# A gelu that waits for VectorE moves behind a seed copy, and convolution items are dealt out otherwise

## The chip, the cores and the metric

The kernel runs on one NeuronCore of a Trainium2 chip. The metric is the device time of one execution in microseconds; the median of three runs is given. The engines that matter here are TensorE (PE in the profile, with PEld for its weight loads), ScalarE (ACT), VectorE (DVE) and SyncE (SP), which issues most transfers.

## The reference

A causal convolution along the sequence, seven taps, with one softmax-normalised set of taps for each of eight groups of 24 channels, is followed by a two-layer network with a quick gelu between its layers:

```python
# x: (8, 4096, 192), weight: (8, 7), w_in: (192, 2048), w_out: (2048, 192)
w = softmax(weight, axis=-1)
out[b, s, h, :] = sum_k w[h, k] * x_pad[b, s + k, h, :]   # 6 zero rows ahead
h = out.reshape(32768, 192) @ w_in
g = h * (1.0 / (1.0 + np.exp(-1.702 * h)))
return g @ w_out
```

## The kernel before

The 32768 tokens are worked on in 32 blocks ("big"), each of which serves two steps `s` (64 steps, numbered from 0). Step 0 is written out by itself and also prepares the weights; the loop runs steps 1 to 63. Both matrix products are done blockwise with seven products in place of eight (a scheme of Strassen's kind), so sums and differences of blocks are formed before and after the products. In the loop a step has two units `a` and `b` (halves of the hidden columns). A unit's products p1 to p7 go to PSUM tiles: `x` and `z` are two of three rotating slots, and `sums` is one tile that both units share.

```python
# cut: inside class Unit
def p1(self):    self.pe(self.x, W11, C11, True)
def seed(self):  act.copy(sums, self.x)             # ScalarE: PSUM to PSUM
def p6(self):    self.pe(sums, X2, V2)              # accumulates on the seed
def keep2(self): self.u2 = ...; act.copy(self.u2, sums)
def p5(self):    self.pe(self.z, X1, V1, True)
def p5b(self):   self.pe(self.z, W23, C32)
def p7(self):    self.pe(sums, X3, V3)
def keep3(self): self.u3 = ...; act.copy(self.u3, sums)
def p2(self):    self.pe(self.x, W12, C21); self.pe(self.x, W13, C31)
def h11(self):   self.gelu(B11, self.x)
def p4(self):    self.pe(sums, W22, V4); self.pe(sums, W23, C31)
def h21(self):   self.gelu(B21, sums)               # reads sums: p4 must be done
def add22(self): vec.tensor_add(self.u3, self.u3, self.z)
def h22(self):   self.gelu(B22, self.u3)            # add22 must be done
def p3(self):    self.pe(self.z, X4, C22); self.pe(self.z, X5, C32)
def add12(self): vec.tensor_add(self.u2, self.u2, self.z)
def h12(self):   self.gelu(B12, self.u2)
def sum_g(self, i): ...                             # VectorE: differences of gelus
```

The convolution of a coming block is done on VectorE between the other operations. It is a list of small items, and `work(n)` takes the next n of them from the list (all of them for None):

```python
def prepare(big):
    for c in range(NC):                  # NC = 3
        yield lambda c=c: transpose_x(big, c)
    if big + 1 < N_BIG:
        yield lambda: load_x(big + 1)
    yield lambda: new_f(big)
    for c in range(NC):
        for k in range(K):               # K = 7; k = 0 is the cheaper form
            yield lambda c=c, k=k: conv(big, c, k)
    for i in range(4):
        yield lambda i=i: sums_c(big, i)
    yield lambda: cross(big)             # a transfer between halves of f
```

The loop, cut to the parts that matter (`nxt` is the first unit of the coming step, whose p1 and seed are done ahead from step 2 on):

```python
for s in range(1, N_ST):
    a, b = nxt or Unit(s, 0), Unit(s, 1)
    if nxt is None:                      # steps 1 and 2
        a.p1(); a.seed(); a.p5(); a.p5b(); a.p6(); a.keep2()
        a.p2(); a.h11(); a.p7(); b.p1(); a.keep3()
    else:
        a.p6(); a.keep2(); a.p2(); a.h11(); a.p7(); a.keep3(); a.p5(); a.p5b()
    nxt = ...
    work(4 if s > 1 else 9)
    a.add22(); a.h22(); a.p4(); a.h21()
    if s > 2: b.p1()
    b.seed(); a.p3()
    work(None if s % 2 and s > 1 else 2)
    a.add12(); b.p5(); b.p6(); b.keep2(); a.h12()
    b.p2(); b.p7(); b.keep3(); b.h11()
    if nxt: nxt.p1()
    b.p5b()
    work(1 if s > 1 else 2)
    a.sum_g(0); a.sum_g(1)
    b.add22(); b.p4(); b.h21(); b.h22()
    if nxt: nxt.seed()
    b.p3(); a.sum_g(2); a.sum_g(3); b.add12(); b.h12()
    if s == 1: work(1)
    if s % 2 and (s + 3) // 2 < N_BIG:
        todo += prepare((s + 3) // 2)
    output(s, b, work)
```

`output` does the second multiplication: five products of 32 matmuls and one of eight "quarters", with `work(2)`, `work(2)`, `work(3)` and `work(3)` between its parts. Its last part, with its lines in the profile:

```python
    work(3)
    p7, p4c = product2(ra, 0, (S3, T3), (A22, T4, 1))    # L476
    act.copy(chunk(p4, 1), p4c)                          # L566
    vec.tensor_add(u1, u1, p7)                           # L567
    vec.tensor_add(u2, u2, p7)                           # L568
    out.turn(1, 1, u1)
    vec.tensor_sub(u2, u2, p4)                           # L570
    out.turn(1, 0, u2)
    out.store()
```

In step 2 the PSUM slot `ra` of step 1's output is the `z` that a's p5 writes.

Of the kernel before, what the change touches and what calls it, by code (L numbers as in the profile page):

```python
# [15 lines left out]
def kernel(  # L16
# [45 lines left out]
    N_BIG = (B // 2) * CHUNKS  # L62
# [27 lines left out]
    def load_x(big):  # L90


        p, c = divmod(big, CHUNKS)
        xin = xins[big] = xin_pool.tile([P, 2, NJ, XW], F32, name="xin")
        if c == 0:
            nc.gpsimd.memset(xin[0:R, :, 0, :], 0.0)
        for o in range(2):
            j = 1 if c == 0 and o == 0 else 0
            t = c * TOK + o * T + (j - 1) * Q
            for v in range(2):  # L100
                q0 = o * R + v * Q
                for n in range(2):
                    nc.sync.dma_start(
                        out=xin[q0 : q0 + Q, n, j:NJ, :],
                        in_=x_v[n, p, t : t + (NJ - j) * Q, v * Q : v * Q + XW].rearrange(
                            "(j i) d -> i j d", i=Q
                        ),
                    )
# [213 lines left out]
    def transpose_x(big, c):  # L322
        if big not in xts:
            xts[big] = xt_pool.tile([P, NC, 2, XT], F32, name="xt")
        vec.transpose(
            xts[big][:, c, :, :].rearrange("p n (j t) -> p (n j) t", t=Q),
            xins[big].rearrange("p n j d -> p (n j) d")[:, :, c * R : c * R + Q],
        )
        if c == NC - 1:
            xins.pop(big)  # L330
# [4 lines left out]
    def conv(big, c, k):  # L335
        src = conv_src(big, c, k)
        dst = fs[big][:, 0, 2 * c : 2 * c + 2, :]
        tap = cw[:, c, k : k + 1]
        if k == 0:
            vec.tensor_scalar_mul(dst, src, tap)  # L340
        else:
            vec.scalar_tensor_tensor(  # L342
                out=dst, in0=src, scalar=tap, in1=dst, op0=ALU.mult, op1=ALU.add
            )

    def sums_c(big, i):
        f = [fs[big][:, 0, j, :] for j in range(NB)]
        dst, a, b = [(V1, C12, C11), (V3, C22, C12), (V2, C22, V1), (V4, C21, V2)][i]
        vec.tensor_sub(f[dst], f[a], f[b])

    def cross(big, b0=0, b1=NB, queue=nc.sync):

        f = fs[big]
        for o in range(2):
            queue.dma_start(out=f[halves[1 - o], 1, b0:b1, :], in_=f[halves[o], 0, b0:b1, :])

    def new_f(big):
        fs[big] = f_pool.tile([P, 2, NB, T], F32, name="f")
# [9 lines that stand above are left out]
            for k in range(K):  # L368
# [3 lines that stand above are left out]
        yield lambda: cross(big)  # L372
# [97 lines left out]
    def product2(slot, bank, ab, last, first=True):  # L470

        dst = slot[:, bank, 0:T]
        tiles = [(c, *ab, c) for c in range(NC)] + [(NC, *last)]
        for j in range(NK):
            for l, a, b, c in tiles:
                nc.tensor.matmul(  # L476
                    dst[l * Q : (l + 1) * Q, :],
                    w_out_s[:, a, j, c * Q : (c + 1) * Q],
                    g[:, b, j, :],
                    start=(first and j == 0),  # L480
                    stop=(j == NK - 1),
                    skip_group_check=True,
                )
        return dst[0 : NC * Q, :], dst[NC * Q :, :]

    def quarters(slot, bank, a, b, c):

        dst = [slot[l * Q : (l + 1) * Q, bank, 0:T] for l in range(4)]
        for i in range(NK // 4):
            for l in range(4):  # L490
                j = NK // 4 * l + i
                nc.tensor.matmul(  # L492
                    dst[l],
                    w_out_s[:, a, j, c * Q : (c + 1) * Q],
                    g[:, b, j, :],
                    start=(i == 0),
                    stop=(i == NK // 4 - 1),
                    skip_group_check=True,
                )
        return dst  # L500
# [28 lines left out]
    def chunk(t, c):  # L529
        return t[c * Q : (c + 1) * Q, :]  # L530

    def output(s, last, work):

        ra, rb = last.x, last.z
        out = Out(s)
        u1, u2, p3, p4 = (
            u_pool.tile([NC * Q, T], F32, name=f"u{i}") for i in range(4)
        )

        p1, p3c = product2(ra, 0, (A11, B11), (S4, B22, 0))  # L540
        act.copy(u1, p1)
        act.copy(chunk(p3, 0), p3c)
        for i in range(4):
            last.sum_g(i)
        p2, p3c = product2(rb, 0, (A12, B21), (S4, B22, 1))
        act.copy(chunk(p3, 1), p3c)  # L546
        work(2)
        vec.tensor_add(u2, u1, p2)
        out.turn(0, 0, u2)
        work(2)  # L550
        p6, p3c = product2(ra, 1, (S2, T2), (S4, B22, 2))
        act.copy(chunk(p3, 2), p3c)  # L552
        vec.tensor_add(u2, u1, p6)
        work(3)
        p5, p4c = product2(rb, 1, (S1, T1), (A22, T4, 0))
        q = quarters(rb, 0, A22, T4, 2)
        act.copy(chunk(p4, 0), p4c)  # L557
        vec.tensor_add(u1, u2, p5)  # L558
        act.copy(chunk(p4, 2), q[2])
        vec.tensor_add(p3, u1, p3)  # L560
        out.turn(0, 1, p3)
        for l in (0, 1, 3):
            vec.tensor_add(chunk(p4, 2), chunk(p4, 2), q[l])  # L563
# [10 lines that stand above are left out]
    todo = []  # L574

    def work(n=None):
        for _ in range(len(todo) if n is None else min(n, len(todo))):
            todo.pop(0)()
# [119 lines left out]
    for s in range(1, N_ST):  # L698
        a, b = nxt or Unit(s, 0), Unit(s, 1)
        if nxt is None:  # L700
            a.p1()
            a.seed()
            a.p5()
            a.p5b()
            a.p6()
            a.keep2()
            a.p2()
            a.h11()
            a.p7()
            b.p1()  # L710
            a.keep3()
        else:
            a.p6()
            a.keep2()
            a.p2()
            a.h11()
            a.p7()
            a.keep3()
            a.p5()
            a.p5b()  # L720
        nxt = Unit(s + 1, 0) if s + 1 < N_ST and s != 1 else None
        work(4 if s > 1 else 9)
        a.add22()
        a.h22()
        a.p4()
        a.h21()
        if s > 2:
            b.p1()
        b.seed()
        a.p3()  # L730
        work(None if s % 2 and s > 1 else 2)
        a.add12()
        b.p5()
        b.p6()
        b.keep2()
        a.h12()
        b.p2()
        b.p7()
        b.keep3()
        b.h11()  # L740
        if nxt:
            nxt.p1()
        b.p5b()
        work(1 if s > 1 else 2)
        a.sum_g(0)
        a.sum_g(1)
        b.add22()
        b.p4()
        b.h21()
        b.h22()  # L750
        if nxt:
            nxt.seed()
        b.p3()
        a.sum_g(2)
        a.sum_g(3)
        b.add12()
        b.h12()
        if s == 1:
            work(1)
        if s % 2 and (s + 3) // 2 < N_BIG:  # L760
            todo += prepare((s + 3) // 2)
        output(s, b, work)


# [28 lines left out]
```

## Time and profile before

| | |
|---|---|
| time, median of three runs | 2455.46 us (2455.34 to 2455.71) |
| span in the profile | 2454.0 us |
| VectorE busy | 1837.9 us (75%) |
| ScalarE busy | 1064.9 us (43%) |
| gelu from SBUF, 128x1024 (L402) | 1057 ns, 252 of them |
| add22 (L449), 128x1024 | 1216 ns, 126 of them |
| seed (L412), 128x1024 | 1007 ns, 126 of them |
| conv item (L342), 128x512 | 748 ns, 564 of them |
| transposes of x (L325), 128x576 | 747 ns, 96 of them |

A line of the profile names the source line, the engine, the operation, what it writes and reads, and how many instructions are merged in it. Each fp32 matmul of the program appears as two records, so that one product of the first kind, with four matmuls, is x8, and one of the second kind, with 32, is x64. L379 is the first multiplication, L476 the second (L492 its quarters), L342 and L340 are conv items, L325 transposes of x, L349 the sums of f, L449 add22, L459 add12, L402 every gelu, L412 the seed, L419 keep2 and L432 keep3.

### The profile page before, as it was taken

What the parts mean: (1) busy time and instruction counts of PE and PEld (TensorE: products, weight loads), DVE (VectorE), ACT (ScalarE), POOL (GpSimd) and SP (SyncE); (2) the same over time, 40 slices, a digit from 0 to 9 for tenths busy, and PEclk for the clock granted to TensorE, in tenths of its full rate; (3) what the DMA queues carried; (4) which work ended last, traced back from release to release, by engine and by line L of the source; (5) the groups of instructions that cost most, each with busy time, mean ns of one, the idle gap of its engine ahead of it and who ended that gap; (6) DMA issues with size and microseconds to landing.
All of it is one profiled execution on the core that took longest, in us unless ns stands there. A gap on an engine that the chain in (4) does not pass through costs nothing.

```text
span 2454.0 us, 71535 instructions
## 1 busy us (share of the span) xinstructions
PE 2434.3 (99%) x32882; PEld 1780.8 (73%) x32882; DVE 1837.9 (75%) x2600; ACT 1064.9 (43%) x1370; POOL 7.5 (0%) x27
## 2 busy tenths in 40 slices
PE   9999999999999999999999999999999999999999
PEld 6767777777677776777777777767777677777776
DVE  8787777777777778777777777787777877777855
ACT  5434344444443443444434444434344344453443
POOL 1000000000000000000000000000000000000000
PEclk9999999999999999999999999999999999999999
DMA  7321222212122121222122221212212122212010
GB/s 176 78 49 37 43 47 58 50 34 58 33 58 58 34 52 32 58 57 51 35 46 44 58 52 34 58 33 56 58 37 49 35 56 58 52 34 48 18 34 15
DMA packets 191421, 120.81 MB, mean 49 GB/s; under 512 B 109904, under 2 KB 185296, under 8 KB 187152
## 3 DMA queue, kind: packets, MB, share of 16 engines
q1 hardware_dynamic: 190272, 115.32, 22.3%
q8 instruction: 257, 4.21, 0.7%
q0 software_dynamic: 288, 0.79, 0.1%
q14 instruction: 44, 0.36, 0.1%
q10 hardware_dynamic: 560, 0.13, 0.0%
HBM read 53.15 MB, written 25.17 MB: 32 GB/s over the span
## 4 chain that ended last, share of the span: by engine, by line
PE 80%; DVE 13%; ACT 4%; issue 2%; DMA 0%; SPq 0%; DVEq 0%; ACTq 0%
PE slot L476 41%; PE slot L379 23%; PE sums L379 14%; DVE f L342 5%; PE slot L492 2%; ACT g L402 2%; DVE u L449 2%; DVE osb L510 2%; DVE u L563 2%; ACT sums L412 1%; DVE u L560 1%; DVE u L567 1%; DVE u L558 1%; PE slot L587 1%; DVE f L340 1%
## 5 line engine op out<-in xcount | busy, mean ns | idle before, releaser
L476 PE MATMUL slot<-g,w_out_s 128*32 128x256 f32 x20544 | 1133.3, 379 | 0.0
L476 PEld LDWEIGHTS slot<-g,w_out_s 128*32 128x32 f32 x20544 | 661.1, 110 | 451.1 <-issue 21.2
L379 PE MATMUL slot<-f,w_in_s 64*128 64x256 f32 x7200 | 847.0, 377 | 2.5 <-DVE u L568 1.7
L468 DVE TENSOR_TENSOR g<-g 128x1024 f32<-128x1024 f32 x504 | 600.2, 1222 | 227.8 <-ACT g L402 223.4
L379 PEld LDWEIGHTS slot<-f,w_in_s 64*128 64x128 f32 x7200 | 690.9, 187 | 95.7 <-DVE u L449 7.5
L379 PE MATMUL sums<-f,w_in_s 64*128 64x256 f32 x4080 | 515.6, 381 | 6.4 <-ACT sums L412 5.3
L379 PEld LDWEIGHTS sums<-f,w_in_s 64*128 64x128 f32 x4080 | 388.2, 187 | 86.6 <-issue 25.1
L342 DVE SCALAR_TENSOR_TENSOR f<-xt,cw,f 128x512 f32<-128x512 f32 x564 | 421.6, 748 | 13.1
L402 ACT ACTIVATE g<-u 128x1024 f32<-128x1024 f32 x252 | 266.5, 1057 | 168.2 <-DVE u L449 154.2
L459 DVE TENSOR_TENSOR u<-u,slot 128x1024 f32<-128x1024 f32 x126 | 153.5, 1218 | 114.7 <-PE slot L379 114.7
L419 ACT COPY u<-sums 128x1024 f32<-128x1024 f32 x126 | 127.6, 1013 | 146.0 <-PE sums L379 146.0
L449 DVE TENSOR_TENSOR u<-u,slot 128x1024 f32<-128x1024 f32 x126 | 153.2, 1216 | 38.0 <-PE slot L379 33.6
L402 ACT ACTIVATE g<-sums 128x1024 f32<-128x1024 f32 x128 | 130.1, 1016 | 95.9 <-PE sums L379 95.9
L402 ACT ACTIVATE g<-slot 128x1024 f32<-128x1024 f32 x132 | 135.6, 1028 | 46.1 <-PE slot L379 46.1
L432 ACT COPY u<-sums 128x1024 f32<-128x1024 f32 x126 | 127.3, 1010 | 35.3 <-PE sums L379 35.3
L558 DVE TENSOR_TENSOR u<-u,slot 96x256 f32<-96x256 f32 x63 | 26.3, 417 | 142.7 <-ACT u L557 142.7
L557 ACT COPY u<-slot 32x256 f32<-32x256 f32 x63 | 23.2, 368 | 248.8 <-PE slot L492 248.8
L412 ACT COPY sums<-slot 128x1024 f32<-128x1024 f32 x126 | 126.9, 1007 | 2.9 <-PE slot L379 0.7
L510 DVE STREAM_TRANSPOSE osb<-u 96x256 f32<-96x256 f32 x253 | 111.1, 439 | 6.9 <-ACT u L690 0.4
L552 ACT COPY u<-slot 32x256 f32<-32x256 f32 x63 | 23.1, 367 | 194.3 <-PE slot L476 194.3
L546 ACT COPY u<-slot 32x256 f32<-32x256 f32 x63 | 23.2, 369 | 170.3 <-PE slot L476 170.3
L566 ACT COPY u<-slot 32x256 f32<-32x256 f32 x63 | 23.2, 368 | 141.0 <-PE slot L476 141.0
(87 smaller groups left out, 678.7 us busy)
## 6 DMA issues: line engine op xcount, KB each, us to landing
xin<-in_x_dram SPq DMA_DIRECT2D x240, 180.0 KB, 4.4
f<-f SPq DMA_DIRECT2D x62, 576.0 KB, 4.7
out_dram<-osb SPq DMA_DIRECT2D x382, 64.0 KB, 1.8
g<-in_moe_w_in_dram SPq DMA_DIRECT2D x8, 384.0 KB, 9.4
g<-in_moe_w_out_dram SPq DMA_DIRECT2D x4, 768.0 KB, 4.9
xin<-in_x_dram SPq DMA_DIRECT2D x16, 160.0 KB, 3.5
f<-f POOLq DMA_DIRECT2D x6, 128.0 KB, 5.6
f<-f SPq DMA_DIRECT2D x2, 192.0 KB, 3.5
```

What stands on the lines that cost most here:

```text
L342: vec.scalar_tensor_tensor(out=dst, in0=src, scalar=tap, in1=dst, op0=ALU.mult, op1=ALU.add)
L379: nc.tensor.matmul(slot[:, h, j * T : (j + 1) * T], w_in_s[halves[h], u, a, j * P : (j + 1) * P], f[halves[h], 0 if h == o else 1, b, :], ...
L402: act.activation(g[:, b, j : j + NK // NU, :].rearrange("p f t -> p (f t)"), src.rearrange("p h n -> p (h n)"), AF.Gelu_apprx_sigmoid,)
L412: act.copy(sums, self.x)
L419: act.copy(self.u2, sums)
L432: act.copy(self.u3, sums)
L449: vec.tensor_add(self.u3, self.u3, self.z)
L459: vec.tensor_add(self.u2, self.u2, self.z)
L468: vec.tensor_sub(v[dst], v[a], v[b])
L476: nc.tensor.matmul(dst[l * Q : (l + 1) * Q, :], w_out_s[:, a, j, c * Q : (c + 1) * Q], g[:, b, j, :], start=(first and j == 0), stop=(j == ...
L510: vec.transpose(self.osb[:, n, :, m * Q : (m + 1) * Q], src.rearrange("p (j t) -> p j t", t=Q),)
L558: vec.tensor_add(u1, u2, p5)
```

## The change

ScalarE takes h21 and the second unit's seed first and h22, which waits for VectorE's add22, after them. The order is meant to keep the seed, on which b's p6 waits, from standing behind add22. Besides that, the items are dealt out otherwise. In steps 4 and up three items go ahead of add22 instead of four, and in even steps three instead of two ahead of add12. Step 3 has six ahead of add22, step 2 seven. In step 1 the list of block 2 is appended after the output and no longer before it, so that its transposes are done in step 2.

```diff
         nxt = Unit(s + 1, 0) if s + 1 < N_ST and s != 1 else None
-        work(4 if s > 1 else 9)
+
+        work({1: 9, 2: 7, 3: 6}.get(s, 3))
         a.add22()
-        a.h22()
         a.p4()
         a.h21()
         if s > 2:
             b.p1()
         b.seed()
+        a.h22()
         a.p3()
-        work(None if s % 2 and s > 1 else 2)
+        work(None if s % 2 and s > 1 else 3)
         a.add12()
 # ... (cut)
         if s == 1:
             work(1)
-        if s % 2 and (s + 3) // 2 < N_BIG:
-            todo += prepare((s + 3) // 2)
+        coming = prepare((s + 3) // 2) if s % 2 and (s + 3) // 2 < N_BIG else ()
+        if s > 1:
+            todo += coming
         output(s, b, work)
+        if s == 1:
+            todo += coming
```

## The prediction

> **What bounds the kernel now.** I read the table of engines first, then the chain that ended last in order of time, then the timelines of TensorE, ScalarE and VectorE for one pair of steps, and last the three early steps.
>
> ```profile
> PE 2434.3 (99%) x32882; PEld 1780.8 (73%) x32882; DVE 1837.9 (75%) x2600; ACT 1064.9 (43%) x1370; POOL 7.5 (0%) x27
> ```
>
> TensorE is the bound. The 99% can't say how much it still loses, since ends of matmuls are modelled; the starts can. A step is cut at the start of the 256-matmul block of the second multiplication. In the TensorE timeline these blocks start at 205.17, 242.64 and 280.60, so the odd step 5 takes 37.47 us and the even step 6 takes 37.96. The same cut through the whole run gives 37.47 for every odd step from 5 to 63 and 37.97 for every even one from 4 to 60 (step 16: 38.24); step 62, which has no conv items left, takes 37.47. Steps 1, 2 and 3 take 42.28, 40.84 and 39.24. The matmuls of all even and odd steps are the same, so an even step loses 0.50 us. Where, the timelines of TensorE, ScalarE and VectorE in step 6 show (start, duration, then the instruction; in brackets the idle time before it):
>
> ```profile
> 267.92 3.68 PE L379 MATMUL slot<-f,w_in_s 64*128 64x256 f32 x32
> 271.77 1.13 PE L379 MATMUL sums<-f,w_in_s 64*128 64x256 f32 x8 [0.17 <-ACT sums L412]
> ```
> ```profile
> 268.71 1.06 ACT L402 ACTIVATE g<-u 128x1024 f32<-128x1024 f32 x1 [2.98 <-DVE u L449]
> 269.68 1.01 ACT L402 ACTIVATE g<-sums 128x1024 f32<-128x1024 f32 x1
> 270.72 1.00 ACT L412 COPY sums<-slot 128x1024 f32<-128x1024 f32 x1
> ```
> ```profile
> 266.28 0.48 DVE L340 TENSOR_SCALAR f<-xt,cw 128x512 f32<-128x512 f32 x1
> 266.80 0.75 DVE L342 SCALAR_TENSOR_TENSOR f<-xt,cw,f 128x512 f32<-128x512 f32 x1
> 267.47 1.21 DVE L449 TENSOR_TENSOR u<-u,slot 128x1024 f32<-128x1024 f32 x1
> ```
>
> Read it backwards. b's p6 starts at 271.77, because it accumulates on sums and the seed copy (L412) ends at 271.72. The seed stands behind h21 and h22 on ScalarE, and h22 could only start when add22 (L449) was done; add22 stood behind four conv items. In step 5 the x32 block starts at 230.45 and p6 at 233.90, 3.45 later; here it is 3.85. That is 0.40; p6 then takes 0.97 to its successor (271.77 to 272.74) and not 0.87 as in step 5, the missing 0.10.
>
> The early steps lose more, to other things (VectorE's timeline, then TensorE's):
>
> ```profile
> 105.19 2.10 DVE L325 STREAM_TRANSPOSE xt<-xin 128x576 f32<-128x576 f32 x3
> 107.31 0.42 DVE L567 TENSOR_TENSOR u<-u,slot 96x256 f32<-96x256 f32 x1
> 107.65 0.41 DVE L568 TENSOR_TENSOR u<-u,slot 96x256 f32<-96x256 f32 x1
> ```
> ```profile
> 108.21 2.00 PE L379 MATMUL slot<-f,w_in_s 64*128 64x256 f32 x16 [1.68 <-DVE u L568]
> ...
> 161.83 1.77 PE L379 MATMUL slot<-f,w_in_s 64*128 64x256 f32 x13 [0.58 <-DMA f<-f]
> ```
>
> Step 2's p5 reuses the PSUM slot of p7 and waits for L567 and L568, which stand behind three transposes of block 2. Step 3's look-ahead p1 waits for the transfer between halves of block 2's f.
>
> **What the skill says.** The Trainium skill, Perfetto Trace Analysis, section Tensor Engine Instruction (MATMUL, LD_WEIGHTS), says that TensorE's end times are estimates of the profiler and that VectorE and ScalarE are strict FIFO. The trace agrees: the seed's input (b's p1) was complete near 268.9, yet it started at 270.72, straight behind the two gelus. So its place in program order is what counts. The Trainium skill, ScalarE: Activation LUTs, section Table sets: the hidden batching unit, says that cheap functions such as copy lie in every table set and that a change of set costs a table load. The trace shows two loads in all, both before the loop, though gelus and copies alternate: the swap should cost no load. The same page, section What ACT_TABLE_LOAD costs, gives every function the same rate per element; here 1.06 us (gelu from SBUF) and 1.00 (copy) for the same 1024 columns agree roughly, so it does not matter which of the two stands first, only what each waits for.
>
> **The change part by part.** No matmul, activation or vector operation is added or removed; only orders move.
>
> Even steps 4 to 60 (29 of them). ScalarE now does h21, seed, h22. h21 needs only p4, whose last matmul ends at 268.08, and ScalarE starts about 0.04 after such an end (240.98 to 241.02 in step 5): 268.12. The seed starts 1.04 later as now, 269.16, and ends 270.16; b's p1 is complete by then. p6 is due at 267.92 + 3.45 = 271.37, so its wait falls with 1.2 us to spare, and the 0.10 with it. Ahead of add22 there are three conv items, not four, so add22 starts at about 266.80 and ends at 268.01; p3, which overwrites the slot that add22 reads, is due at 267.92 + 0.86 = 268.78. No new wait. Gain 0.50 each, 29 x 0.50 = 14.5 us. Odd steps from 5 on have no wait there; their fourth item was only the issue of the transfer, so VectorE's order is unchanged: 0.
>
> Step 1: p6 started at 78.28 behind a seed that ended at 78.23. The order of ScalarE brings the seed one gelu (0.97) earlier; p6 is due at 77.95. 0.33 + 0.10 = 0.43 us. The waits of p4 and p3 for keep3 and add22 stay.
>
> Step 2: block 2's items are appended only after the output of step 1, so the three transposes come after L567 to L570. L567 can start when p7 ends (105.46), about 105.5; L568 starts 0.34 later, takes 0.41, and ends at 106.26. p5 is due 0.97 after p1's start (the spacing in step 5): 106.36. So 108.21 - 106.36 = 1.85 us. The transposes then fill idle time: VectorE waited 4.44 us before the next add22.
>
> Step 3: block 2's list has 31 items (3 transposes, load, new f, 21 convs, 4 sums, transfer). Before, step 1's output takes 3 of them and step 2 takes 4 + 2 + 1 + 10, so 20 are done when step 3 begins; after, step 2 takes 7 + 3 + 1 + 10 = 21. Step 3's first stretch then has six, not four: five convs (0.745 each from the trace's spacing) and one sum (0.40). VectorE gets to them at 149.81, so add22 starts at 149.81 + 3.73 + 0.40 = 153.94 and ends at 155.16, not 154.01. p3 is due at 153.24 + 0.86 = 154.10: a new wait of 1.1 us, and 0.10 on resuming. Against it: p6 no longer waits (it would have been due at 156.69 and starts at 157.10 now; after, 155.20 + 2.69 = 157.89), and the transfer is issued behind three more sums at 156.35, not 157.11; at its 4.68 us it lands at 161.03, while the look-ahead p1 comes at 157.89 + 3.46 = 161.35. From p6 to the end of the step a smooth step takes 8.74 (233.90 to 242.64), so it ends at 166.63, where it ended at 167.20. 0.57 us.
>
> Sum: 14.5 + 0.43 + 1.85 + 0.57 = 17.35 us. 2455.46 - 17.35 = 2438.1.
>
> **Rivals.** First: the wait only moves, to p3 behind add22, in the even steps. Then about 0.06 of the gap (now in the x32 block, 3.68 against 3.62) stays and the time is near 2440; the spare 0.77 us speaks against more. Second: h22, now last, delays keep2 and so h12, the two sums of g, b's add22 and b's p3. That chain has little room: keep2 at 235.03, add22 done at 240.65, p3 at 240.81. But h22 would end near 271.2 and p6 near 272.4, so keep2 isn't touched. If it were, by 0.3 or so, the even steps would keep most of their 37.97 and the odd ones get worse: 2450 to 2460. In odd steps h22 ends at about 233.7 before keep2 at 235.03. Third: the conv moved behind add22 delays add12. Three convs from 267.95 end at 270.2; add12 waits for p3 until about 270.6. A small margin, but enough; if wrong, add12 comes 0.3 late, hidden behind keep2. Fourth: step 3 pays more than it gains, because the transfer lands late although issued earlier. Then 2439.
>
> **Range and chances.** The steady term is 29 equal repetitions, so it is nearly all or nothing; the three early steps add at most a microsecond of doubt each. Range 2436 to 2442. All that lies above 37.47 is 14.5 us in the even steps and 4.81 + 3.37 + 1.77 in steps 1 to 3 (where more matmuls account for part), 24.5 us or 1.0%, so 2% faster is out of reach; 2% slower would need 49 us, 0.8 per step, which I see nowhere. Hence 0.98 for within 2% and 0.01 for either side.
>
> **What would show it.** In the profile after: even steps at 37.47 like the odd ones; the seed ending near 1.2 us ahead of p6; no TensorE wait on L412; step 2 shorter by 1.85 with p5 close behind p1; in step 3 a wait of p3 for L449 of about 1.1 us and none for the transfer. I'd be wrong if even steps stay above 37.6, with keep2, add22 or add12 named as releasers, or if odd steps rise.

## The result, and the profile after

The changed kernel takes 2438.45 us (median of 6 runs, 2438.28 to 2438.89) against 2455.42 us for the kernel before (6 runs, 2455.27 to 2455.71): a ratio of 0.9931, 95% interval 0.9918 to 0.9944. The prediction was 2438.1 us.

The table of engines and the chain that ended last, of the changed kernel:

```profile
PE 2423.5 (99%) x32882; PEld 1786.0 (73%) x32882; DVE 1837.7 (75%) x2600; ACT 1064.9 (44%) x1370; POOL 7.5 (0%) x27
...
PE 97%; DVE 2%; DMA 1%; ACT 0%; issue 0%; SPq 0%; ACTq 0%
```

The first line looks like that of before: busy shares tell nothing here. The second one does: in the kernel before, TensorE had 80% of that chain, VectorE 13% and ScalarE 4%. Now the chain runs along TensorE nearly all the way.

Step 6 in the changed kernel, in the timelines of TensorE, ScalarE and VectorE (start, duration, instruction):

```profile
265.53 3.62 PE L379 MATMUL slot<-f,w_in_s 64*128 64x256 f32 x32
268.98 1.03 PE L379 MATMUL sums<-f,w_in_s 64*128 64x256 f32 x8
```
```profile
265.74 1.02 ACT L402 ACTIVATE g<-sums 128x1024 f32<-128x1024 f32 x1 [2.39 <-PE sums L379]
266.80 1.00 ACT L412 COPY sums<-slot 128x1024 f32<-128x1024 f32 x1
267.71 1.06 ACT L402 ACTIVATE g<-u 128x1024 f32<-128x1024 f32 x1
```
```profile
263.91 0.48 DVE L340 TENSOR_SCALAR f<-xt,cw 128x512 f32<-128x512 f32 x1
264.31 1.21 DVE L449 TENSOR_TENSOR u<-u,slot 128x1024 f32<-128x1024 f32 x1
265.44 2.32 DVE L342 SCALAR_TENSOR_TENSOR f<-xt,cw,f 128x512 f32<-128x512 f32 x3
268.33 1.22 DVE L459 TENSOR_TENSOR u<-u,slot 128x1024 f32<-128x1024 f32 x1 [0.57 <-PE slot L379]
```

The seed ends at 267.80, 1.18 us ahead of p6 at 268.98, and p6 follows the x32 block after 3.45 us with no idle time in brackets. The prediction had 1.2 us to spare. h22, now last, runs to 268.77, well ahead of keep2, which starts at 270.12.

Here are the steps, counted as in the prediction from one first matmul of the second multiplication to the next; "lead-in" is all that comes before step 1.

| us | before | after | difference | predicted |
|---|---|---|---|---|
| lead-in (step 0, same program) | 44.84 | 44.61 | -0.24 | 0 |
| step 1 | 42.28 | 41.83 | -0.45 | -0.43 |
| step 2 | 40.84 | 39.45 | -1.39 | -1.85 |
| step 3 | 39.24 | 39.44 | +0.20 | -0.57 |
| an even step, 4 to 60 | 37.97 | 37.46 | -0.50 | -0.50 |
| steps 4 to 63 together | 2262.71 | 2247.74 | -14.97 | -14.5 |

Every one of steps 4 to 63 now takes 37.46 us. Of the 14.97 us, 0.27 is step 16, which was longer by that much in the profile of before. Two of the ten further profiles show the same in step 16, the other eight not, so it comes and goes with the run. The lead-in varies by itself: in the twelve profiles of this study, all with the same lead-in, it takes 44.57 to 45.20 us. So a difference of a few tenths between two profiles' spans means little, and the steps are compared instead.

Two of the early steps missed. In step 2, p5 still waits (VectorE's, ScalarE's and TensorE's timelines of the changed kernel):

```profile
105.24 0.42 DVE L567 TENSOR_TENSOR u<-u,slot 96x256 f32<-96x256 f32 x1 [0.75 <-ACT u L566]
105.58 0.41 DVE L568 TENSOR_TENSOR u<-u,slot 96x256 f32<-96x256 f32 x1
```
```profile
104.84 0.37 ACT L566 COPY u<-slot 32x256 f32<-32x256 f32 x1 [2.24 <-PE slot L476]
```
```profile
106.14 2.00 PE L379 MATMUL slot<-f,w_in_s 64*128 64x256 f32 x16 [0.30 <-DVE u L568]
```

L567 did not start when p7 ended (104.77); it waited for ScalarE's copy L566 of another part of the same slot.

In step 3 the wait of p3 for add22 came as predicted, but the transfer took 5.64 us instead of 4.68 (TensorE's timeline, then two entries of the chain):

```profile
153.13 2.86 PE L379 MATMUL slot<-f,w_in_s 64*128 64x256 f32 x24 [0.93 <-DVE u L449]
```
```profile
154.26 5.64 DMA f<-f
...
159.96 1.77 PE slot L379 x13
```

### The profile page after: what moved, and what is told of

Same layout as the page of the kernel before. It is cut to its first block, busy times and chain, and to the rows that moved or that the text cites. A ratio compares the mean times of both kernels' runs of the same rounds, so it can differ in the third digit from the quotient of the medians.

```text
span 2437.2 us, 71539 instructions
## 1 busy us (share of the span) xinstructions
PE 2423.5 (99%) x32882; PEld 1786.0 (73%) x32882; DVE 1837.7 (75%) x2600; ACT 1064.9 (44%) x1370; POOL 7.5 (0%) x27
## 4 chain that ended last, share of the span: by engine, by line
PE 97%; DVE 2%; DMA 1%; ACT 0%; issue 0%; SPq 0%; ACTq 0%
PE slot L476 45%; PE slot L379 31%; PE sums L379 18%; PE slot L492 2%; DVE f L342 1%; DMA f<-f 0%; DMA xin<-in_x_dram 0%; DVE u L449 0%; DVE osb L510 0%; SPq L103 0%; ACT g L402 0%; DVE g L468 0%; DVE xt L325 0%; ACT u L419 0%; DVE f L349 0%
## 5 line engine op out<-in xcount | busy, mean ns | idle before, releaser
L419 ACT COPY u<-sums 128x1024 f32<-128x1024 f32 x126 | 127.5, 1012 | 133.2 <-PE sums L379 133.2
L566 ACT COPY u<-slot 32x256 f32<-32x256 f32 x63 | 23.1, 366 | 141.1 <-PE slot L476 141.1
```

## The experiments

Each kernel differs from the changed kernel, or where said from the kernel before, by a few lines. Times are medians; the step lengths are from each one's profile.

### The ScalarE order alone

```diff
# kernel before
         a.add22()
-        a.h22()
         a.p4()
         a.h21()
...
         b.seed()
+        a.h22()
         a.p3()
```

> The kernel before with the ScalarE order alone (h21, seed, h22); items dealt as before. Theory A, the order alone frees the seed: even steps 4 to 60 go from 37.97 to about 37.53 (the 0.06 stays with which p3 waits for add22 behind four items), step 1 from 42.28 to 41.83, steps 2 and 3 as before (40.84, 39.24), about 2442 us. Rival B, the fourth item ahead of add22 is what costs, and the order does nothing by itself: even steps stay at 37.97, about 2455 us.

Measured: 2442.7 us, ratio to before 0.9946 (0.9932 to 0.9961). Even steps 37.54, step 1 41.83, step 2 40.86, step 3 39.24. TensorE in step 6:

```profile
267.01 3.70 PE L379 MATMUL slot<-f,w_in_s 64*128 64x256 f32 x32
270.54 1.03 PE L379 MATMUL sums<-f,w_in_s 64*128 64x256 f32 x8
```

VectorE's add22 in the same step:

```profile
266.58 1.21 DVE L449 TENSOR_TENSOR u<-u,slot 128x1024 f32<-128x1024 f32 x1
```

Rival B falls: the order alone takes away p6's wait. What remains is 0.08 us in the x32 block (3.70 against 3.62), where p3 stands behind add22, which here ends at 267.79 (266.58 + 1.21), just as p3 is due (267.01 + 0.86 = 267.87). The profile names no releaser for so short a wait; it is inferred from these times and from the next run, where add22 ends earlier and the x32 block is back at 3.46 us before p6.

### The dealing alone

```diff
# changed kernel
         a.add22()
+        a.h22()
         a.p4()
         a.h21()
...
         b.seed()
-        a.h22()
         a.p3()
```

> The changed kernel with the old ScalarE order (h22, h21, seed); items dealt as in the changed kernel. Theory A, only the order frees the seed: even steps at 37.9 or so, about 2453 us. Rival B, one item less ahead of add22 is enough: add22 ends at the step's 268.01, so h22 runs to 269.1, h21 to 270.1 and the seed to 271.1, 0.3 us ahead of p6 (271.37); even steps at 37.46, step 1 back at 42.28, about 2439 us.

Measured: 2439.48 us, ratio to before 0.9932 (0.9917 to 0.9947). Even steps 37.46, step 1 42.27, step 2 39.45, step 3 39.08. ScalarE and TensorE in step 6:

```profile
265.94 1.06 ACT L402 ACTIVATE g<-u 128x1024 f32<-128x1024 f32 x1 [2.19 <-DVE u L449]
266.91 1.01 ACT L402 ACTIVATE g<-sums 128x1024 f32<-128x1024 f32 x1
267.94 1.00 ACT L412 COPY sums<-slot 128x1024 f32<-128x1024 f32 x1
```
```profile
269.39 1.03 PE L379 MATMUL sums<-f,w_in_s 64*128 64x256 f32 x8
```

So theory A in its "only the order" form falls too. The seed is still last of three, but since add22 ends one item earlier it ends at 268.94, 0.45 us before p6 at 269.39. Either half of the change recovers the even steps by itself: the order 0.42 of 0.50 us, the dealing all of it. They are not a sum; the second finds nothing left. What the order brings besides is a larger margin (1.18 us and not 0.45), step 1 (42.27 against 41.83), whose dealing ahead of add22 the change left alone, and part of step 3. There add22 stands behind six items, and with the old order p6 still waits for the seed:

```profile
156.90 1.14 PE L379 MATMUL sums<-f,w_in_s 64*128 64x256 f32 x8 [0.17 <-ACT sums L412]
```

The changed kernel has no such wait there. Its step 3 took 38.67 us in a profile with nearly the same landing of the transfer (4.75 us after its issue, here 4.81; see the repeat below), against 39.08 here, so the order is worth about 0.41 us in step 3.

### Block 2's list ahead of the output again

```diff
# changed kernel
-        work({1: 9, 2: 7, 3: 6}.get(s, 3))
+        work({1: 9, 2: 4, 3: 6}.get(s, 3))
...
-        if s > 1:
-            todo += coming
+        todo += coming
         output(s, b, work)
-        if s == 1:
-            todo += coming
```

> The changed kernel with block 2's list appended ahead of step 1's output, as before, and four items (not seven) in step 2's first stretch, so that only the three transposes move. Theory: they come ahead of L567 and L568 again, p5 waits for them, step 2 goes from 39.45 back to 40.84: 2439.8 us. Rival, the transposes were hidden and step 2's gain comes from the extra conv item: step 2 stays at 39.45, 2438.4 us.

Measured: 2439.37 us, ratio 0.9932 (0.9917 to 0.9947). Step 2 takes 40.50, not 40.84, and step 3 38.55. The edit did not do exactly what was meant. One item fewer of block 1 was left when the output began than in the kernel before, so one of the three transposes fell earlier and only two stood ahead of L567 (VectorE's and TensorE's timelines):

```profile
104.49 1.44 DVE L325 STREAM_TRANSPOSE xt<-xin 128x576 f32<-128x576 f32 x2
105.96 0.42 DVE L567 TENSOR_TENSOR u<-u,slot 96x256 f32<-96x256 f32 x1
```
```profile
106.86 2.00 PE L379 MATMUL slot<-f,w_in_s 64*128 64x256 f32 x16 [1.04 <-DVE u L568]
```

That makes it a finer test: the spacing from p1's last start to p5's first, 0.21 in smooth running, is 2.06 us with three transposes (kernel before), 1.42 with two, 0.67 with none. The third one costs 0.64, close to its duration of 0.70 (2.10 for three). The first two cost 0.75 together and not 1.40, because L567 could not have started for part of that time anyway: without transposes it starts 0.47 us after p7's end. The rival (a hidden transpose) falls, and 0.46 (0.67 - 0.21) remain that have nothing to do with transposes. Step 3's 38.55 also differs in dealing: 22 items are done before it, not 21.

### Four items ahead of add22 in step 3

```diff
-        work({1: 9, 2: 7, 3: 6}.get(s, 3))
+        work({1: 9, 2: 7, 3: 4}.get(s, 3))
```

> The changed kernel with four items (not six) ahead of add22 in step 3. The transfer of block 2's f is issued after the same work as now. Theory A, step 3 is bound by the landing of that transfer: p3's wait of 1.1 us goes, the look-ahead p1 waits that much longer, step 3 stays near 39.4 (38.9 if the transfer takes 4.7 us here and not 5.6), 2438 us. Rival B, p3's wait for add22 is the loss: step 3 falls to 38.3, 2437.3 us.

Measured: 2438.16 us, ratio 0.9927 (0.9911 to 0.9944); step 3 38.47. p3's wait of 1.1 us went (a spacing of 0.29 remains), and the look-ahead p1 waited for the transfer instead (a spacing of 0.62; TensorE's timeline):

```profile
158.29 0.59 PE L379 MATMUL slot<-f,w_in_s 64*128 64x256 f32 x2
159.13 1.78 PE L379 MATMUL slot<-f,w_in_s 64*128 64x256 f32 x13 [0.24 <-DMA f<-f]
```

The step's end is at 164.50, 6.21 us after this p1's start; in the repeat of the changed kernel below, where p1 does not wait, it is 5.28 us (159.66 to 164.94). So 0.93 us are lost to the transfer, more than the bracket says. In this profile the transfer landed 4.68 us after its issue, as in the kernel before. Theory A's sizes were 39.4, or 38.9 with the quick transfer; rival B's was 38.3. By the number alone B is nearer, but the wait for the transfer that A named is there. The repeat below separates the two.

### Both of these again

> The changed kernel once more, to see whether step 3's transfer is late each time. Theory A: a 16 KB transfer of the instruction queue is under way when the second half of the transfer is issued, because TensorE reaches a fixed place of its stream then; the issue takes about 2.6 us again, the first half lands 5.6 us after its issue, step 3 takes 39.4. Rival B: it was chance; issue 0.6 us, landing in 4.7 us, step 3 near 38.7.

> Four items in step 3's first stretch once more. Theory A: without p3's wait TensorE is 1.2 us further on and the instruction transfer is over when the second half is issued: issue 0.6 us, landing 4.7 us after the issue, step 3 at 38.5. Rival B: chance; in a repeated run issue and landing differ.

Measured: the changed kernel 2438.44 us (0.993, 0.9914 to 0.9946), step 3 38.67; four items 2438.27 us (0.9931, 0.9917 to 0.9945), step 3 38.45. In the repeated profile of the changed kernel p3 waits as before and the look-ahead p1 does not (TensorE's timeline; the x16 at 159.66 follows p7 at 158.79 with the usual spacing):

```profile
153.51 2.86 PE L379 MATMUL slot<-f,w_in_s 64*128 64x256 f32 x24 [0.93 <-DVE u L449]
...
158.79 1.03 PE L379 MATMUL sums<-f,w_in_s 64*128 64x256 f32 x8
159.66 1.89 PE L379 MATMUL slot<-f,w_in_s 64*128 64x256 f32 x16
```

38.67 is what the prediction computed (166.63 - 127.96). So the 39.44 of the first profile comes from a late landing, which this kernel can show or not. Against the same landing, four items are worth 0.2 us (38.45 against 38.67): the 1.1 us that p3 no longer waits are spent again, nearly all, on the transfer. That is theory A's mechanism, and rival B's 1.1 us falls.

In these profiles the landing goes with how long an issue took. The transfer is issued in two halves, and the look-ahead p1 waits for the first. The columns are: start of a 16 KB transfer of the instruction queue, issue of the second half, how long that issue took (all in us from step 3's start), and step 3's length.

| kernel | instructions | second half | issue took | step 3 |
|---|---|---|---|---|
| before | 27.22 | 29.66 | 0.59 | 39.24 |
| order alone | 27.23 | 29.68 | 0.59 | 39.24 |
| four items | 27.10 | 28.89 | 0.59 | 38.47 |
| four items, again | 27.22 | 28.89 | 0.59 | 38.45 |
| after | 28.35 | 28.89 | 2.64 | 39.44 |
| after, again | 28.40 | 28.90 | 1.65 | 38.67 |
| dealing alone | 28.26 | 28.88 | 1.71 | 39.08 |

The instruction transfers take 1.0 to 1.4 us. In all twelve profiles, the issue of this second half took 0.59 where that transfer was over by then and 1.65 to 2.79 where it was not. The first half landed 4.66 to 4.68 us after its own issue in the four profiles with 0.59, after 4.75 and 4.81 in the two with 1.65 and 1.71, and after 5.20 to 5.66 in the six with 2.59 to 2.79. (The 39.08 of the dealing alone is therefore not a late landing, but the wait for the seed shown above.)

So the prediction's third term, that the landing takes 4.68 us as before, was not safe. In all twelve profiles the instruction transfer starts 1.04 to 1.28 us after the end of step 3's first add22, on which p3 waits. The two items added ahead of add22 move that end from 26.05 to 27.18 us after the step's start, and the instruction transfer moves with it, onto the issue. Theory A of the repeat is right about the coincidence and wrong that it always delays the landing: with 1.65 it hardly did. That the one causes the other was not tried in isolation and stays argued, and why an overlapped issue took now 1.7 us and now 2.6 stays open.

### The additions of p7 ahead of ScalarE's copy

```diff
# output(), all steps
-        act.copy(chunk(p4, 1), p4c)
         vec.tensor_add(u1, u1, p7)
         vec.tensor_add(u2, u2, p7)
+        act.copy(chunk(p4, 1), p4c)
```

> The changed kernel with the two additions of p7 (L567, L568) written ahead of ScalarE's copy of p4's chunk (L566) in the output, all steps. Theory A: in the changed kernel L567 waits for L566 and not for p7, which costs p5 0.47 us in step 2; then step 2 falls from 39.45 to 38.98 and nothing else changes, 2438.0 us. Rival B: L567 starts 0.47 late for another reason (the matmul's end reaches VectorE later): step 2 stays at 39.45.

Measured: 2533.29 us, ratio 1.0314 (1.0299 to 1.033), 3% slower, from the exchange of one line with two. Even steps take 39.32, odd ones 38.87; step 2 is at 39.42. Neither theory said so. The waits of this kernel (in this file the additions are L566 and L567 and the copy L568; total us, times, longest):

```profile
ACT u L568 <- DVE u L567: 299.0, 63, 5.1
...
PEld sums L379 <- ACT u L419: 103.4, 59, 2.0
PE sums L379 <- ACT u L419: 79.7, 59, 1.6
```

Step 2 of it, ScalarE's and TensorE's timelines:

```profile
105.93 0.37 ACT L568 COPY u<-slot 32x256 f32<-32x256 f32 x1 [3.08 <-DVE u L567]
```
```profile
106.35 2.00 PE L379 MATMUL slot<-f,w_in_s 64*128 64x256 f32 x16 [0.26 <-ACT u L568]
```

Step 6 of it, the same timelines:

```profile
265.21 0.37 ACT L568 COPY u<-slot 32x256 f32<-32x256 f32 x1 [5.10 <-DVE u L567]
265.61 1.01 ACT L419 COPY u<-sums 128x1024 f32<-128x1024 f32 x1
```
```profile
262.22 1.14 PE L379 MATMUL sums<-f,w_in_s 64*128 64x256 f32 x8
...
266.67 1.13 PE L379 MATMUL sums<-f,w_in_s 64*128 64x256 f32 x8 [1.59 <-ACT u L419]
```

The three readers of the slot are one chain in the built program, in the order of the source, although they only read, two of them on one engine and one on another. Exchanging them moved the wait from VectorE to ScalarE. Whether the chip needs this order or only the program's builder sets it, no run here shows. In step 2 L567's wait for ScalarE indeed went (the additions start 0.07 us after p7's end), but the copy now came last and p5 waited for that, so p5's spacing is 0.63 and not 0.67. Theory A's premise, that L567 waits for L566, is shown; its conclusion was wrong because the slot is only free when the last of the three is done. In the other steps the additions stand behind three conv items, so the copy waits up to 5.1 us and keeps keep2 (L419) waiting behind it, and p7 waits for keep2. This is the strict order of ScalarE's queue that the Trainium skill states (Perfetto Trace Analysis, section Tensor Engine Instruction (MATMUL, LD_WEIGHTS)): keep2's input was complete when p6 ended, at about 263.4, and it ran at 265.61.

### h22 behind keep2

```diff
         b.seed()
-        a.h22()
         a.p3()
...
         b.keep2()
+        a.h22()
         a.h12()
```

> The changed kernel with h22 moved once more, behind b's keep2 and ahead of h12. It puts one gelu (0.97 us) into the chain keep2, h12, two sums of g, b's add22, b's p3, of which the trace shows 0.16 us to spare. Theory: each loop step loses 0.8 to 0.9 us, 62 steps, 2488 to 2495 us. Rival: the chain has more room than that, ScalarE is only 44% busy, and the time stays within 2 us of 2438.4.

Measured: 2498.3 us, ratio 1.0172 (1.0157 to 1.0187); steps 4 to 63 take 38.41 each except step 16 (38.69), 0.95 more than in the changed kernel. In step 6, ScalarE, VectorE and TensorE:

```profile
274.67 1.01 ACT L419 COPY u<-sums 128x1024 f32<-128x1024 f32 x1 [2.32 <-PE sums L379]
275.58 2.00 ACT L402 ACTIVATE g<-u 128x1024 f32<-128x1024 f32 x2
```
```profile
277.62 2.48 DVE L468 TENSOR_TENSOR g<-g 128x1024 f32<-128x1024 f32 x2 [2.85 <-ACT g L402]
280.02 1.21 DVE L449 TENSOR_TENSOR u<-u,slot 128x1024 f32<-128x1024 f32 x1
```
```profile
281.29 2.00 PE L379 MATMUL slot<-f,w_in_s 64*128 64x256 f32 x16 [0.68 <-DVE u L449]
```

The two gelus in a row delay the sums of g, these delay b's add22, and b's p3 waits for it. One gelu of 0.97 us in that place costs 0.95 us per step; the room was near zero, less than the 0.16 that had been read off, and the expected 0.8 to 0.9 (2488 to 2495 us) was a little low. The danger that the prediction's second rival named was real, then: the chain from keep2 to p3 has almost no room. The change put h22 into a gap before keep2, where it costs nothing.

### Ten and three items in steps 2 and 3

```diff
-        work({1: 9, 2: 7, 3: 6}.get(s, 3))
+        work({1: 9, 2: 10, 3: 3}.get(s, 3))
```

> The changed kernel with ten items (not seven) in step 2's first stretch, where VectorE idles 2.4 us, and three (not six) in step 3's. Theory: the three convs fit the idle time; in step 3 add22 comes in time and the transfer is issued 2.2 us earlier and lands before the look-ahead p1 even if it takes 5.6 us: step 3 falls from 39.44 to 37.46, 2436.5 us. Rival: add22 of step 2 comes late and p3 waits there: step 2 rises by what step 3 gains less, 2437.5 to 2438.5 us.

Measured: 2437.16 us, ratio 0.9923 (0.9906 to 0.9939). Step 2 39.45, step 3 37.46, as every later step. The steps are as expected; the time lies 0.66 us above the expected 2436.5, which was reckoned from the late landing (39.44). Reckoned from 38.67, it is 2437.2. The second half's issue took 2.79 us here, and the landing 5.20 us, and did no harm: the issue came at 26.92 and not 28.89. The three convs went into VectorE's idle time in step 2, which had been 2.41 us ahead of add22.

### The early steps put right

```diff
# changed kernel
             a.seed()
+            if s > 1:
+                b.p1()
             a.p5()
-            a.p5b()
+            if s == 1:
+                a.p5b()
             a.p6()
...
             a.p7()
-            b.p1()
+            if s == 1:
+                b.p1()
+            else:
+                a.p5b()
             a.keep3()
...
-        work({1: 9, 2: 7, 3: 6}.get(s, 3))
+        work({1: 8, 2: 10}.get(s, 3))
...
-        work(None if s % 2 and s > 1 else 3)
+        work({1: 4}.get(s, None if s % 2 else 3))
```

> A version meant to be faster than both: the changed kernel with ten and three items in the first stretches of steps 2 and 3; in step 1 eight items and four in the two stretches (not nine and three); in step 2 b's p1 is put ahead of a's p5, whose slot is not yet free, and p5b takes b's p1's old place ahead of p4. Theory: step 2 falls from 39.45 to about 38.95, because b's p1 fills the wait for the slot; step 1 from 41.83 to 41.5, because add22 is ready when p3 comes; step 3 at 37.46: 2436.3 us. Rival: the early steps are bound elsewhere (keep3 ahead of p4) and the lost time turns up there: 2437.2 us as with ten items alone.

Measured: 2436.31 us, ratio to before 0.9922 (0.9909 to 0.9935). In the same comparison the changed kernel took 2438.44, so this version beats both. Steps 1, 2 and 3 take 41.50, 38.90 and 37.47. TensorE in step 2, where p1, b's p1 and p5 now run as one block without a wait:

```profile
104.64 2.86 PE L379 MATMUL slot<-f,w_in_s 64*128 64x256 f32 x24
107.34 1.03 PE L379 MATMUL sums<-f,w_in_s 64*128 64x256 f32 x8
...
112.12 2.00 PE L379 MATMUL sums<-f,w_in_s 64*128 64x256 f32 x16 [0.30 <-ACT u L432]
```

Here the wait for the slot was filled and not shortened. The last line, p4 behind keep3, stays as it was, so the rival falls: nothing turned up there.

## Why the prediction was right, and where it was not

The total is off by 0.35 us of a change of 17. It is closer than its parts, and that is in part luck: in the two profiles compared above, steps 2 and 3 gave 1.23 us less than said, and the lead-in (0.24), step 16 (0.27) and the other steps from 4 on (0.20) gave 0.71 more, none of which the prediction had.

**Even steps: right in size, right in mechanism, too narrow in its cause.** Predicted 0.50 us each and 14.5 in all; measured 0.50 and 14.97 over steps 4 to 63, 0.27 of it step 16. The times that carry the working hold: the seed 1.2 us ahead (1.18), add22 done before p3, the 0.10 gone with the wait. But the text gave the gain to ScalarE's order, with the item taken from add22 as what keeps p3 free. The two runs with one half each show that the item alone brings all of it, and the order alone all but 0.08.

**Step 1: right** (0.43 said, 0.45 measured), and due to the order alone: 42.27 without it.

**Step 2: the mechanism right, a term mis-sized.** The step that failed is "L567 can start when p7 ends (105.46), about 105.5". It starts 0.47 us after p7's end, because the built program has it wait for ScalarE's copy of the same slot. 1.85 became 1.39. That these three reads are chained is shown by the exchange, which turned the wait around.

**Step 3: the chance in the sum.** p3's new wait (1.1 us) and the issue of the transfer (28.37 us after the step's start; the prediction's 156.35 - 127.96 = 28.39) came as said. "At its 4.68 us it lands" failed in the first profile: 5.64 us, and the fourth rival happened, a transfer landing late although issued earlier. In the second profile of the same kernel the landing was in time (4.75 us) and the step took 38.67, the predicted figure to the hundredth. So the term is -0.57 or +0.20 from profile to profile; how often it is the one or the other, two profiles do not tell.

**The rivals.** The first (the wait moves to p3) is what the order alone shows, at 0.08 us and not 0.06. The second was rightly set aside, and its danger is now measured. The third did not occur: in step 6 add12 starts at 268.33 after 0.57 us of waiting for p3, with the three convs over.

## What to carry to other kernels

Where an engine waits on a chain through two others, find every member of the chain that could be moved and count the slack after each move alone: two cures of one wait need not add up. Here the second bought only margin in the even steps. Before an instruction is put behind another on a strict queue, follow what stands behind it there; the same gelu was free in one gap and cost 0.95 us per step one place later. Readers of one PSUM slot on different engines may be chained by the program, so read off who waits for whom before trusting that a reader starts when its data is ready.

## What had not been expected of the hardware

The order of two reads of one slot, on ScalarE and VectorE, was worth 95 us (2533.29 against 2438.45), through the built program's waits and the engines' strict queues. The issue of the second half of step 3's transfer on SyncE took 0.59 us or 1.65 to 2.79 us, the longer times where a 16 KB transfer of instructions was under way, in all twelve profiles; the first half's landing moved from 4.7 us to at most 4.8 in two of these and to 5.2 or more in six. It is no rule for every issue: in the changed kernel the first half, issued at 154.26, took 0.47 us with the same instruction transfer just begun. And TensorE, after a wait, needed about 0.10 us more for its first matmuls (p6 of step 6 before: a spacing of 0.31 and not 0.21 between starts), so a wait cost that much beyond its length. The same 0.31 stands at the first matmuls behind each second multiplication in the changed kernel, 63 times, where nothing is waited for.
